# Converting float64 weights to float32 by a scaled copy, shifts and masks, in a fused attention and two-MLP kernel

## The chip, the cores and the metric

The kernel runs on 1 core of one Trainium2 chip. The metric is device time in microseconds: before the change the median of 3 runs is 858.35 us (858.0 to 858.82). Lower is better.

## What is computed

Attention in chunks of 64 tokens (4 batches, 8 heads, 576 tokens, head size 64), then a SiLU MLP (512 to 2048 to 512), then a gated MLP (512 to 1536 to 512), on 2304 tokens. All five weight matrices arrive as float64, and the kernel converts them itself.

```python
scores = scale * np.matmul(q_c, k_c.transpose(0, 1, 2, 4, 3))
attn = np.exp(scores - max); attn = attn / (sum + 1e-09); x = attn @ v_c
h = x @ w_in
x = (h * (1.0 / (1.0 + np.exp(-h)))) @ w_out
out = ((x @ w_a) * (x @ w_b)) @ w_out2
```

## The kernel before

Everything is written out by hand in program order: each engine runs its own instructions in the order in which the source emits them, and nothing is reordered.

**Weights.** A weight block is 128 x 512 float64 (512 KB). There are 68: 32 for the first MLP (16 slices m of the hidden layer, `w_in[m]` and `w_out[m]` in turn, numbered 0 to 31 here, so that block 2m is `w_in[m]`), and 36 for the second. `fetch` (L128) loads a block into one of two raw buffers through SP's queue. `exponents` (L140) takes the sign on ACT, masks the exponent on DVE and rescales it on ACT; `mantissa` (L154) and `begin` (L170) build the mantissa on DVE; `powers` (L182) and `upper` (L187) multiply both together on DVE. For a block of the first MLP `upper` then also rounds the result to the matmul's format on ACT (the upper half, L202), and `lower` (L205) subtracts on DVE what the upper half lost (the lower half, L209). Blocks of the second MLP are written back to DRAM instead. `weights` (L212) chains one block's fetch and opening with the later stages of the block before it.

**Steps.** The first MLP is a loop over steps k; step k = m works on slice m for the first main block of 512 tokens. In one step PE does, in order: the product of slice k+1 with the tokens, `front(k+1)` (12 matmuls of 512 columns: four each of xhi with the upper half of the weights, xlo with the upper half, xhi with the lower half, L384); `side_back(k)` and `side_front(k+1)`, the same work for a side block of 256 tokens, which runs along in the first 16 steps; and `back(k)`, the product with `w_out[k]` (L423). ACT evaluates SiLU on each front twice (L404 and L405), DVE subtracts (L401). Each step calls `prep_a`, and so `weights`, twice: once between `side_back` and `side_front`, once between `side_front` and `back`. Attention for later token tiles is threaded through the steps by a table of steps (`plan`): with the tiles begun at steps 2, 5, 8 and 11 the softmax's exponential falls into steps 3, 6, 9 and 12, between `side_front` and the second `prep_a`.

**The start.** Before step 0 six token tiles go through attention in a hand-ordered sequence, into which blocks 0, 1 and 2 are opened; `busy(n)` (L706) puts n filler matmuls on PE. It ends with `front(0)`, `busy(7)` and `back(0)`.

```python
        finish(pend, 0)
        lower()
        begin_a()
        busy(7)
        back(0)
```

**Buffers.** `tmp` is a set of three 128 x 512 float32 tiles that the mantissas share with SiLU's results `g` until step 17, when mantissas move to a pool of their own (`conv`). `at` is a set of five tiles for attention's q, k, v, scores and probabilities.

Of the kernel before, what the change touches and what calls it, by code (L numbers as in the profile page):

```python
# [7 lines left out]

F32 = mybir.dt.float32
F32R = mybir.dt.float32r  # L10
BF16 = mybir.dt.bfloat16
U16 = mybir.dt.uint16
U32 = mybir.dt.uint32
U64 = mybir.dt.uint64
AF = mybir.ActivationFunctionType
# [5 lines left out]
P = 128  # L21
# [3 lines left out]
def chunk_attention_silu_mlp_gated_mlp(  # L25
# [77 lines left out]
    nc.vector.memset(ebias, -8.0 * ((1023 - 127) << 4))  # L103

    def bank(tag, shape):
        return psum.tile(shape, F32, tag=tag, name="ps_" + tag)
# [18 lines left out]
    turn = [0]  # L125
    leaving = []

    def fetch(src):  # L128
        raw = raws[:, turn[0] % 2]
        turn[0] += 1  # L130
        nc.sync.dma_start(out=raw, in_=src)
        fetched.append(raw)
# [7 lines left out]
    def exponents():  # L140

        raw = fetched.pop(0)
        top = raw.bitcast(U16).rearrange("p (f t) -> p f t", t=4)[:, :, 3]
        topb = raw.bitcast(BF16).rearrange("p (f t) -> p f t", t=4)[:, :, 3]
        e = spool.tile([P, DM], U16, tag="e", name="e")
        sg = spool.tile([P, DM], BF16, tag="sg", name="sg")
        nc.scalar.activation(sg, topb, AF.Sign)  # L147
        nc.vector.tensor_scalar(  # L148
            out=e, in0=top, scalar1=0x7FF0, scalar2=None, op0=ALU.bitwise_and
        )  # L150
        nc.scalar.activation(e, e, AF.Relu, scale=8.0, bias=ebias)  # L151
        opened.append([raw.bitcast(U32).rearrange("p (f t) -> p f t", t=2), e, sg])

    def mantissa():  # L154
        w32 = opened[0][0]
        if "conv" in late:
            mant = late["conv"].tile([P, DM], F32, tag="mant", name="mant", bufs=3)
        else:
            mant = spool.tile([P, DM], F32, tag="tmp", name="mant", bufs=3)
        nc.vector.tensor_scalar(  # L160
            out=mant.bitcast(U32),
            in0=w32[:, :, 1],
            scalar1=0xFFFFF,
            scalar2=0x100000,
            op0=ALU.bitwise_and,
            op1=ALU.bitwise_or,
        )
        opened[0].append(mant)

    def begin(dest):  # L170
        w32, e, sg, mant = opened.pop(0)
        nc.vector.scalar_tensor_tensor(  # L172
            out=mant,
            in0=w32[:, :, 0],
            scalar=2.0**-32,
            in1=mant.bitcast(U32),
            op0=ALU.mult,
            op1=ALU.add,
        )
        stage_1.append((dest, mant, sg, e))  # L180

    def powers():  # L182
        if stage_1:
            _, _, sg, e = stage_1[0]
            nc.vector.tensor_tensor(out=sg, in0=sg, in1=e.bitcast(BF16), op=ALU.mult)

    def upper():  # L187
        if not stage_1:
            return
        dest, w, sg, _ = stage_1.pop()  # L190
        nc.vector.scalar_tensor_tensor(  # L191
            out=w, in0=w, scalar=2.0**-20, in1=sg, op0=ALU.mult, op1=ALU.mult
        )
        if dest[0] == "f":
            wf[dest[1:]] = d = dram.tile([P, DM], F32, name=f"wf{dest[1]}{dest[2]}")
            leaving.append((d, w))
            return
        _, m, j = dest
# [24 lines left out]
    def flush():  # L223
        for _ in range(2):
            lower()
            powers()
            upper()
        leave()

# [162 lines left out]
    def front_a(b, m, ptag, pool, later=False):  # L392
        n = width(b)
        ps = bank(ptag, [P, n])
        product(ps, wA[m][0], x_t[b])
        g = spool.tile([P, DM], F32, tag="tmp", name="g", bufs=3)[:, :n]
        ghi = pool.tile([P, n], F32R, tag="ghi", name="ghi")
        glo = pool.tile([P, n], F32R, tag="glo", name="glo")

        def finish():  # L400
# [54 lines left out]
    def comb_load(u):  # L455
        s, mat = divmod(u, 2)
        if u % 2 and u != 3:
            buf = raws.rearrange("p a n -> p (a n)").bitcast(F32)
        else:
            buf = slot("buf", F32)  # L460
        buf = buf.rearrange("p (o n) -> p o n", o=8)
        for m, sl in ((2 * s, slice(1, 3)), (2 * s + 1, slice(0, 8, 7))):
            nc.gpsimd.dma_start(out=buf[:, sl], in_=wf[mat, m].rearrange("p (o n) -> p o n", o=2))
        bufs[u] = buf
# [182 lines left out]
            units_b += [("f", mat, 2 * s), ("f", mat, 2 * s + 1), ("f", 2, 2 * s + mat)]  # L647
    done = [0, 0]

    def begin_a():  # L650
        begin(("a", *units_a[done[0]]))
        done[0] += 1

    def prep_a():
        if done[0] < len(units_a):
            m, j = units_a[done[0]]
            weights((w_in, w_out)[j][m], ("a", m, j))
            done[0] += 1
            return True
        return False  # L660

    def drain():
        leave()
        lower()
        powers()
        upper()

    def prep_b():
        if done[1] < len(units_b):
# [17 lines left out]
    with tc.manual_schedule():  # L687
# [40 lines left out]

        qk_in(0)
        qk_in(1)  # L730
        fetch(w_in[0])
        v_in(0)
        qk_in(2)
        qk_in(3)
        v_in(1)
        v_in(2)
        fetch(w_out[0])
        v_in(3)
        qk_in(4)
        qk_in(5)  # L740
# [83 lines left out]
        S(1)  # L824
        busy(3)
        att_exp(0)
        exponents()
        S(2)
        att_max(1, W, True)
        att_exp(1)  # L830
        mantissa()
        att_norm(0)
        busy(3)
        Tr(0, "at")
# [11 lines left out]
        rest["X", 0]()  # L846
        rest["P", 1]()
        Tr(2, "sB")
        exponents()
        att_norm(3)  # L850
        rest["P", 2]()
        rest["L", 0]()
# [1 line left out]
        S(4)  # L854
        rest["X", 1]()
        att_max(4, W, True)
        begin_a()
        fetch(w_in[1])
# [6 lines left out]
        powers()  # L865
        rest["X", 2]()
        busy(1)
        mantissa()
        upper()
        S(5)  # L870
        att_norm(4)
# [2 lines left out]
        att_max(5, W)  # L874
        Tr(4, "at")
        rest["P", 4]()
        begin_a()
        lower()
        V(3, "sB")
        rest["X", 3]()  # L880
# [3 lines left out]
        V(4, "sA")  # L884
        rest["X", 4]()
        pend[0], silu = front_a(main[0], 0, "mm", gpool, True)
        powers()
        Tr(5, "at")
        rest["L", 4]()
        silu()  # L890
        rest["P", 5]()
        upper()
        exponents()
        busy(2)
        V(5, "mm")
        mantissa()
        finish(pend, 0)
        lower()
        begin_a()
        busy(7)  # L900
        back(0)
        rest["X", 5]()
        powers()
        upper()
        rest["L", 5]()
        prep_a()
# [8 lines left out]
        first = []  # L915

        def enter_b():
            late.pop("conv")
            conv_cm.__exit__(None, None, None)
            att_cm.__exit__(None, None, None)  # L920
            late["b"] = ctx.enter_context(
                tc.tile_pool(name="bpool", bufs=1, side="right", reuse_waits="tile")
            )
            for h in range(2):
                load_pair(0, h)


        def in_last(m, pos):
            if pos == "c":
                if prep_b():  # L930
                    return
                if leaving or stage_1 or stage_2:
# [134 lines left out]
        for k in range(END):  # L1067
# [8 lines left out]
            run(k, "a2")  # L1076
            if k == MA + 1:
                side_cm.__exit__(None, None, None)
                conv_cm = tc.tile_pool(name="conv", bufs=1, side="right", reuse_waits="tile")
                late["conv"] = conv_cm.__enter__()  # L1080
            if k in joint:
                finish(pend, k + 1)
            if k >= L0:
# [250 lines left out]
```

## Time and profile before

| | us |
|---|---|
| median of 3 runs | 858.35 |
| the profiled execution, its own time | 858.17 |
| its span in the profile | 856.4 |
| PE busy | 846.9 |
| DVE busy | 571.4 |
| ACT busy | 440.9 |

The profiled execution took 858.17 us, of which the span of the profile covers 856.4. PE is busy for 99% of it; of the 40 slices of the page only the first and the last show PE busy for less than nine tenths. Mean granted clock of TensorE over the span is 0.997 of full speed.

### The profile page before, as it was taken

The numbers are of one execution on the slowest core, as the hardware profiler recorded it, in microseconds if no ns is written. First come the engines' busy times: TensorE is split into PE (matmuls) and PEld (weight loads), VectorE is DVE, ScalarE is ACT, GpSimd is POOL, SyncE is SP. The second block draws the span as 40 slices with busy tenths as digits, with TensorE's granted clock in tenths as the row PEclk, the third lists the DMA queues.
The fourth block names the chain that finished last, engine by engine and source line by source line (L and its number), as shares of the span: only waits on it lengthen the run. The fifth ranks groups of instructions, "written<-read, shape, count | busy, mean of one in ns | idle before, by whom it ended". The sixth has DMA issues, their size and how long they took to land.

```text
span 856.4 us, 14161 instructions
## 1 busy us (share of the span) xinstructions
PE 846.9 (99%) x5484; PEld 771.6 (90%) x5484; DVE 571.4 (67%) x1097; ACT 440.9 (51%) x837; POOL 50.3 (6%) x91
## 2 busy tenths in 40 slices
PE   8999999999999999999999999999999999999998
PEld 7788888888888888888889999999999999999998
DVE  6996977765677656766865998583554594454563
ACT  6777767745665656545555554363333373333252
POOL 0000000020100100023201110000000000000000
PEclk9999999999999999999999999999999999999999
DMA  7454443355554655457799788878766888666761
GB/s 271 119 179 134 145 152 111 100 181 200 166 187 152 222 172 161 160 184 290 252 364 370 295 314 328 308 293 269 258 258 263 304 299 281 241 250 247 290 227 56
DMA packets 54034, 193.85 MB, mean 226 GB/s; under 512 B 5904, under 2 KB 13584, under 8 KB 45520
## 3 DMA queue, kind: packets, MB, share of 16 engines
q1 hardware_dynamic: 46752, 169.76, 55.6%
q0 software_dynamic: 6928, 22.81, 8.1%
q8 instruction: 43, 0.70, 0.3%
q10 hardware_dynamic: 288, 0.39, 0.1%
q14 instruction: 23, 0.19, 0.1%
HBM read 141.03 MB, written 51.90 MB: 225 GB/s over the span
## 4 chain that ended last, share of the span: by engine, by line
PE 95%; ACT 2%; issue 1%; DVE 1%; DMA 1%; SPq 0%; ACTq 0%
PE ps_acc L980 23%; PE ps_acc L423 20%; PE ps_mm L384 15%; PE ps_sA L384 7%; PE ps_at L980 6%; PE ps_sA L980 6%; PE ps_mm L980 5%; PE ps_sB L980 5%; PE ps_sA L423 2%; PE ps_sB L423 1%; PE ps_at L384 1%; PE ps_at L267 1%; PE ps_at L349 1%; PE ps_at L326 1%; DMA start<-kt 1%
## 5 line engine op out<-in xcount | busy, mean ns | idle before, releaser
L980 PE MATMUL ps_acc<-xo,ring 128*128 128x384 f32 x868 | 168.2, 335 | 0.0
L423 PE MATMUL ps_acc<-ghi,wA 128*128 128x512 f32 x512 | 159.2, 392 | 0.0
L980 PEld LDWEIGHTS ps_acc<-xo,ring 128*128 128x128 f32 x868 | 152.0, 188 | 0.3 <-DVE gq L1055 0.3
L423 PEld LDWEIGHTS ps_acc<-ghi,wA 128*128 128x128 f32 x512 | 94.2, 188 | 19.1
L384 PE MATMUL ps_mm<-xhi,wA 128*128 128x512 f32 (+1 forms) x400 | 100.7, 373 | 0.0
L423 PE MATMUL ps_acc<-glo,wA 128*128 128x512 f32 x256 | 100.0, 390 | 0.0
L384 PEld LDWEIGHTS ps_mm<-xhi,wA 128*128 128x128 f32 x400 | 70.6, 188 | 12.6 <-ACT wA L202 0.2
L401 DVE TENSOR_TENSOR glo<-g,ghi 128x512 fp32r<-128x512 f32 x80 | 50.5, 632 | 31.4 <-ACT ghi L405 31.4
L404 ACT ACTIVATE g<-ps_mm 128x512 f32<-128x512 f32 (+1 forms) x50 | 28.0, 559 | 81.7 <-PE ps_mm L384 76.7
L423 PEld LDWEIGHTS ps_acc<-glo,wA 128*128 128x128 f32 x256 | 48.0, 188 | 10.2
L1114 ACT ACTIVATE u<-gq 128x384 fp32r<-128x384 f32 x84 | 40.6, 516 | 30.4 <-DVE gq L1055 28.6
L1115 DVE TENSOR_TENSOR u<-gq,u 128x384 fp32r<-128x384 f32 x84 | 44.4, 552 | 17.4 <-ACT u L1114 17.0
L980 PE MATMUL ps_acc<-u,ring 128*128 128x384 f32 x272 | 53.6, 337 | 0.3
L151 ACT ACTIVATE e<-e,ebias 128x512 uint16<-128x512 uint16 x68 | 49.1, 722 | 9.1 <-DVE e L148 9.1
L384 PE MATMUL ps_mm<-xlo,wA 128*128 128x512 f32 (+1 forms) x200 | 49.8, 371 | 0.0
L384 PE MATMUL ps_sA<-xhi,wA 128*128 128x512 f32 x184 | 49.6, 391 | 0.0
L980 PEld LDWEIGHTS ps_acc<-u,ring 128*128 128x128 f32 x272 | 47.6, 188 | 1.3 <-ACT gq L989 0.8
L980 PE MATMUL ps_at<-xo,ring 128*128 128x384 f32 x231 | 47.8, 334 | 0.0
L191 DVE SCALAR_TENSOR_TENSOR mant<-mant,sg 128x512 f32<-128x512 f32 x68 | 46.5, 684 | 0.1
L172 DVE SCALAR_TENSOR_TENSOR mant<-raws,mant 128x512 f32<-128x512 uint32 x68 | 46.5, 683 | 0.1
L147 ACT ACTIVATE sg<-raws 128x512 bf16<-128x512 bf16 x68 | 45.7, 672 | 0.6 <-DMA raws<-w_in 0.6
L980 PE MATMUL ps_sB<-xo,ring 128*128 128x384 f32 x220 | 44.9, 334 | 0.0
(185 smaller groups left out, 1490.1 us busy)
## 6 DMA issues: line engine op xcount, KB each, us to landing
ring<-w SPq DMA_DIRECT2D x30, 1024.0 KB, 6.3
ring<-wg SPq DMA_DIRECT2D x24, 1024.0 KB, 4.9
ring<-wg SPq DMA_DIRECT2D x24, 768.0 KB, 5.7
wg<-ring SPq DMA_DIRECT2D x12, 1024.0 KB, 6.6
wf<-mant SPq DMA_DIRECT2D x36, 256.0 KB, 2.2
wg<-ring SPq DMA_DIRECT2D x12, 768.0 KB, 6.4
raws<-w_in SPq DMA_DIRECT2D x16, 512.0 KB, 3.5
raws<-w_out SPq DMA_DIRECT2D x16, 512.0 KB, 3.5
```

Source lines behind the costliest of these rows:

```text
L147: nc.scalar.activation(sg, topb, AF.Sign)
L151: nc.scalar.activation(e, e, AF.Relu, scale=8.0, bias=ebias)
L172: nc.vector.scalar_tensor_tensor(out=mant, in0=w32[:, :, 0], scalar=2.0**-32, in1=mant.bitcast(U32), op0=ALU.mult, op1=ALU.add,)
L191: nc.vector.scalar_tensor_tensor(out=w, in0=w, scalar=2.0**-20, in1=sg, op0=ALU.mult, op1=ALU.mult)
L267: nc.tensor.matmul(soft[i][j % len(soft[i])][n, j, hp, :], lhsT=q[r, hp, n], rhs=k[r, hp, n], start=True, stop=True,)
L384: nc.tensor.matmul(ps, lhsT=a[:, kk * P:(kk + 1) * P], rhs=b[:, kk, :], start=(j == 0 and kk == 0), stop=(j == 2 and kk == KT - 1),)
L401: nc.vector.tensor_tensor(out=glo, in0=g, in1=ghi.bitcast(F32), op=ALU.subtract)
L404: nc.scalar.activation(g, ps, AF.Silu)
L423: nc.tensor.matmul(acc_t[b][j], lhsT=a[:, j * P:(j + 1) * P], rhs=g, start=(m == 0 and i == 0 and (b != SIDE or j % 2 == 0)), stop=(m == M ...
L980: nc.tensor.matmul(ps, lhsT=a, rhs=b, start=first and i == 0, stop=last and i == 2, skip_group_check=True,)
L1114: nc.scalar.activation(hi, src, AF.Copy)
L1115: nc.vector.tensor_tensor(out=lo, in0=src, in1=hi.bitcast(F32), op=ALU.subtract)
```

## The change

**Conversion.** `scaled` makes one ACT instruction of a block: a copy, times 2^111, of the upper 32-bit words of the raw float64, read as float32. `magnitude` multiplies it on DVE by two constants in one instruction and, in a second one in place, shifts left by 3 and masks the sign. `begin` puts the sign bit in from the raw upper words and then the three leading bits of the raw lower words, two DVE instructions in place. `exponents`, `mantissa`, `powers` and the multiplication in `upper` are gone. `upper` keeps only the rounding on ACT, `lower` is as it was.

**Stages.** In `weights` each stage now works on a block one call behind the stage ahead of it: a call that fetches block n scales it at its end, brings block n-1 through `magnitude` and `begin`, and block n-2 through `upper` and `lower`. Before, a call opened and began block n, ran `powers` and `upper` for n-1 and `lower` for n-2.

**Buffers.** There are three raw buffers. `g` no longer takes a `tmp` tile during the first MLP: the side block has a tile of its own, the main block holds one `at` tile until step 17 and uses a pool of two tiles (`gate`) after that; the pool `conv` is gone.

**Fillers.** `busy(7)` ahead of `back(0)` is `busy(2)`.

```diff
-    raws = spool.tile([P, 2, DM], U64, tag="raw", name="raws", bufs=1)
+    raws = spool.tile([P, RAWS, DM], U64, tag="raw", name="raws", bufs=1)
...
+    def scaled():
+        dest, raw = fetched.pop(0)
+        w = spool.tile([P, DM], F32, tag="tmp", name="w", bufs=3)
+        nc.scalar.activation(w, words(raw)[1].bitcast(F32), AF.Copy, scale=2.0**111)
+        opened.append((dest, raw, w))
+
+    def magnitude():
...
+        w = opened[0][2]
         nc.vector.tensor_scalar(
+            out=w, in0=w, scalar1=2.0**-126, scalar2=2.0**-97, op0=ALU.mult, op1=ALU.mult
         )
         nc.vector.tensor_scalar(
+            out=w.bitcast(U32), in0=w.bitcast(U32), scalar1=3, scalar2=0x7FFFFFFF,
+            op0=ALU.logical_shift_left, op1=ALU.bitwise_and,
         )
+    def begin():
...
         nc.vector.scalar_tensor_tensor(
+            out=wu, in0=high, scalar=0x80000000, in1=wu,
+            op0=ALU.bitwise_and, op1=ALU.bitwise_or,
         )
         nc.vector.scalar_tensor_tensor(
+            out=wu, in0=low, scalar=29, in1=wu,
+            op0=ALU.logical_shift_right, op1=ALU.bitwise_or,
         )
...
     def weights(src, dest):
-        fetch(src)
         leave()
-        exponents()
+        fetch(src, dest)
+        upper()
+        magnitude()
+        begin()
         lower()
-        powers()
-        mantissa()
-        upper()
-        begin(dest)
+        scaled()
...
-        g = spool.tile([P, DM], F32, tag="tmp", name="g", bufs=3)[:, :n]
+        if b == SIDE:
+            g = side.tile([P, n], F32, tag="g", name="g")
+        elif "g" in late:
+            g = late["g"].tile([P, n], F32, tag="g", name="g", bufs=2)
+        elif "b" in late:
+            g = spool.tile([P, n], F32, tag="tmp", name="g", bufs=3)
+        else:
+            if "g1" not in late:
+                late["g1"] = late["att"].tile([P, DM], F32, tag="at", name="g")
+            g = late["g1"]
...
-        lower()
-        begin_a()
-        busy(7)
+        magnitude()
+        begin()
+        busy(2)
         back(0)
         rest["X", 5]()
-        powers()
         upper()
         rest["L", 5]()
         prep_a()
         prep_a()
```

How the order of instructions changes, at the three places that matter below. Numbers behind a name tell its tiles apart.

ACT in step 0, before: the product `front(2)` reads the weight tile `wA_698` (block 4), and L202 fills its upper half.

```order
L404 ACTIVATE g_668<-ps_mm_655 128x512
L405 ACTIVATE ghi_669<-ps_mm_655 128x512
L147 ACTIVATE sg_689<-raws_82 128x512
L151 ACTIVATE e_688<-e_688,ebias_80 128x512
L202 ACTIVATE wA_698<-mant_631 128x512
L404 ACTIVATE g_715<-ps_at_702 128x256
L405 ACTIVATE ghi_716<-ps_at_702 128x256
```

ACT in step 0 now: `front(2)` reads `wA_687`, and L196 is the upper half; `g_683` and `ghi_681` are the SiLU of `side_front(1)`.

```order
L399 ACTIVATE g_535<-ps_mm_627 128x512
L400 ACTIVATE ghi_640<-ps_mm_627 128x512
L196 ACTIVATE wA_594<-w_599 128x512
L147 ACTIVATE w_665<-raws_82 128x512
L399 ACTIVATE g_683<-ps_at_668 128x256
L400 ACTIVATE ghi_681<-ps_at_668 128x256
L196 ACTIVATE wA_687<-w_606 128x512
```

The upper half that `front(2)` needs stood ahead of the side block's SiLU and now stands behind it.

ACT in step 3, before: `front(5)` writes `ps_mm_1033` and reads `wA_976` (block 10); L297 is the exponential of attention.

```order
L202 ACTIVATE wA_976<-mant_909 128x512
L404 ACTIVATE g_999<-ps_mm_986 128x256
L405 ACTIVATE ghi_1000<-ps_mm_986 128x256
L297 ACT_TABLE_LOAD
L297 ACTIVATE s_979<-s_979 128x512
L147 ACTIVATE sg_1009<-raws_82 128x512
L151 ACTIVATE e_1008<-e_1008,ebias_80 128x512
L202 ACTIVATE wA_976<-mant_973 128x512
L404 ACT_TABLE_LOAD
L404 ACTIVATE g_1046<-ps_mm_1033 128x512
```

ACT in step 3 now: `front(5)` writes `ps_mm_969` and reads `wA_947`.

```order
L399 ACTIVATE g_940<-ps_mm_925 128x256
L400 ACTIVATE ghi_938<-ps_mm_925 128x256
L283 ACT_TABLE_LOAD
L283 ACTIVATE s_918<-s_918 128x512
L196 ACTIVATE wA_947<-w_857 128x512
L147 ACTIVATE w_954<-raws_82 128x512
L399 ACT_TABLE_LOAD
L399 ACTIVATE g_535<-ps_mm_969 128x512
```

The upper half of block 10 stood ahead of the side block's SiLU, the table load and the exponential, and now stands behind all of them; what stood behind them before was that of block 11, which `back(5)` reads a step later.

DVE at the start, before: the lines ahead of the last `xlo` (L365, from `ps_sB`) that `front(0)` reads.

```order
L286 TENSOR_TENSOR start<-ps_acc_444,mx 128x4x64
L286 TENSOR_TENSOR start<-ps_acc_445,mx 128x4x64
L172 SCALAR_TENSOR_TENSOR mant<-raws,mant 128x512
L209 TENSOR_TENSOR wA<-mant,wA 128x512
L365 TENSOR_TENSOR xlo<-ps_sB,xhi 128x4x128
```

DVE at the same place now, where that `xlo` is L351.

```order
L272 TENSOR_TENSOR start<-ps_acc_437,mx 128x4x64
L272 TENSOR_TENSOR start<-ps_acc_438,mx 128x4x64
L174 SCALAR_TENSOR_TENSOR w<-raws,w 128x512
L178 SCALAR_TENSOR_TENSOR w<-raws,w 128x512
L203 TENSOR_TENSOR wA<-w,wA 128x512
L351 TENSOR_TENSOR xlo<-ps_sB,xhi 128x4x128
```

One more instruction stands ahead of `xlo`, and it reads what the one ahead of it writes.

## Rows read from the trace of the kernel before

**Rows 1.** The page, part 1: busy us, share of the span, instructions.

```profile
PE 846.9 (99%) x5484; PEld 771.6 (90%) x5484; DVE 571.4 (67%) x1097; ACT 440.9 (51%) x837; POOL 50.3 (6%) x91
```

**Rows 2.** Stretches: length, busy PE, PEld, DVE, ACT, POOL, granted clock, DMA.

```profile
30.00:40.00 10.00, 9.49 (x85) 8.20 (x84) 9.93 (x21) 7.34 (x13) 0.00 (x0) 1.00 0.29 76
```

**Rows 3.** Groups by line and form: count, busy us, mean ns, idle before.

```profile
L151 ACT ACTIVATE e<-e,ebias 128x512 uint16<-128x512 uint16 x68 | 49.1, 722 | 9.1 <-DVE e L148 9.1
...
L172 DVE SCALAR_TENSOR_TENSOR mant<-raws,mant 128x512 f32<-128x512 uint32 x68 | 46.5, 683 | 0.1
L147 ACT ACTIVATE sg<-raws 128x512 bf16<-128x512 bf16 x68 | 45.7, 672 | 0.6 <-DMA raws<-w_in 0.6
...
L160 DVE TENSOR_SCALAR mant<-raws 128x512 uint32<-128x512 uint32 x68 | 28.5, 419 | 0.0
...
L202 ACT ACTIVATE wA<-mant 128x512 fp32r<-128x512 f32 x32 | 20.3, 633 | 8.5 <-DVE mant L191 8.5
```

**Rows 4.** Timeline of DVE, steps 2 and 3: start us, us, instruction.

```profile
63.91 0.69 DVE L191 SCALAR_TENSOR_TENSOR mant<-mant,sg 128x512 f32<-128x512 f32 x1
64.51 0.68 DVE L172 SCALAR_TENSOR_TENSOR mant<-raws,mant 128x512 f32<-128x512 uint32 x1
66.32 0.69 DVE L281 TENSOR_REDUCE mx<-ps_at 128x8 f32<-128x512 f32 x1 [1.13 <-PE ps_at L267]
67.05 0.69 DVE L286 TENSOR_TENSOR s<-ps_at,mx 128x512 f32<-128x512 f32 x1
```

**Rows 5.** The chain that ended last, at the start: start us, us, what.

```profile
17.42 0.34 DVE e L148
```

**Rows 6.** Timeline of the start, DVE and PE, up to `back(0)`.

```profile
26.57 0.68 DVE L172 SCALAR_TENSOR_TENSOR mant<-raws,mant 128x512 f32<-128x512 uint32 x1
...
27.77 0.68 DVE L365 TENSOR_TENSOR xlo<-ps_sB,xhi 128x512 fp32r<-128x512 f32 x1
...
28.51 1.20 PE L384 MATMUL ps_mm<-xlo,wA 128*128 128x512 f32 x4
...
32.94 0.68 DVE L209 TENSOR_TENSOR wA<-mant,wA 128x512 fp32r<-128x512 f32 x1
...
33.36 1.83 PE L710 MATMUL ps_sA<-start 128*128 128x128 f32 x14
...
34.95 0.70 PE L423 MATMUL ps_acc<-ghi,wA 128*128 128x512 f32 x2
```

**Rows 7.** Timeline, end of step 0: upper half, last third of `side_front(1)`, `front(2)`.

```profile
44.34 0.64 ACT L202 ACTIVATE wA<-mant 128x512 fp32r<-128x512 f32 x1
44.41 0.64 PE L384 MATMUL ps_at<-xhi,wA 128*128 128x256 f32 x4
...
45.04 1.19 PE L384 MATMUL ps_mm<-xhi,wA 128*128 128x512 f32 x4
```

**Rows 8.** Timeline, step 3: last third of `side_front(4)`, ACT, then `front(5)`.

```profile
68.70 0.64 PE L384 MATMUL ps_mm<-xhi,wA 128*128 128x256 f32 x4
...
69.66 0.38 ACT L405 ACTIVATE ghi<-ps_mm 128x256 fp32r<-128x256 f32 x1
70.06 1.28 ACT L297 ACT_TABLE_LOAD   x1
71.35 0.63 ACT L297 ACTIVATE s<-s 128x512 f32<-128x512 f32 x1
71.89 0.65 ACT L147 ACTIVATE sg<-raws 128x512 bf16<-128x512 bf16 x1
...
71.91 1.07 PE L384 MATMUL ps_mm<-xhi,wA 128*128 128x512 f32 x4
```

**Rows 9.** Tile k, POOL's loads; timeline of PE, transposes, then the next scores.

```profile
DMA to landing us min/median/max: 3.2/3.8/6.1
...
80.28 0.60 PE L326 MATMUL ps_at<-ident,s 128*128 128x128 f32 x4
...
86.26 0.68 PE L267 MATMUL ps_at<-k,q 64*64 64x64 f32 x16
```

More of the change, by code (lines that the diff above doesn't have):

```diff
@@ L126, in chunk_attention_silu_mlp_gated_mlp, with fetch @@
     leaving = []
-    def fetch(src):
-        raw = raws[:, turn[0] % 2]
+    def fetch(src, dest):
+        raw = raws[:, turn[0] % RAWS]
         turn[0] += 1
         nc.sync.dma_start(out=raw, in_=src)
-        fetched.append(raw)
+        fetched.append((dest, raw))
     def leave(n=0):
@@ L138, in leave, with words @@
             nc.sync.dma_start(out=dst, in_=src)
[L140 to L147, printed above, removed]
+    def words(raw):
+        w32 = raw.bitcast(U32).rearrange("p (f t) -> p f t", t=2)
+        return w32[:, :, 0], w32[:, :, 1]
@@ L148, in exponents @@
+    def scaled():
[4 more added lines that the diff above has]
+    def magnitude():
+        if not opened:
+            return
+        w = opened[0][2]
         nc.vector.tensor_scalar(
-            out=e, in0=top, scalar1=0x7FF0, scalar2=None, op0=ALU.bitwise_and
+            out=w, in0=w, scalar1=2.0**-126, scalar2=2.0**-97, op0=ALU.mult, op1=ALU.mult
@@ L150, in exponents @@
         )
[L151 to L159, printed above, removed]
-        nc.vector.tensor_scalar(
[L161 to L166, printed above, removed]
-        )
-        opened[0].append(mant)
@@ L170, in begin @@
-    def begin(dest):
-        w32, e, sg, mant = opened.pop(0)
-        nc.vector.scalar_tensor_tensor(
[L173 to L178, printed above, removed]
-        )
[L180 to L190, printed above, removed]
+        nc.vector.tensor_scalar(
+            out=w.bitcast(U32),
+            in0=w.bitcast(U32),
+            scalar1=3,
+            scalar2=0x7FFFFFFF,
+            op0=ALU.logical_shift_left,
+            op1=ALU.bitwise_and,
+        )
@@ L191, in upper @@
+    def begin():
+        if not opened:
+            return
+        dest, raw, w = opened.pop(0)
+        low, high = words(raw)
+        wu = w.bitcast(U32)
+        nc.vector.scalar_tensor_tensor(
+            out=wu, in0=high, scalar=0x80000000, in1=wu,
+            op0=ALU.bitwise_and, op1=ALU.bitwise_or,
+        )
         nc.vector.scalar_tensor_tensor(
-            out=w, in0=w, scalar=2.0**-20, in1=sg, op0=ALU.mult, op1=ALU.mult
+            out=wu, in0=low, scalar=29, in1=wu,
+            op0=ALU.logical_shift_right, op1=ALU.bitwise_or,
@@ L196, in upper @@
             leaving.append((d, w))
+        else:
+            stage_1.append((dest, w))
+    def upper():
+        if not stage_1:
             return
+        dest, w = stage_1.pop()
         _, m, j = dest
@@ L212, in weights @@
     def weights(src, dest):
-        fetch(src)
         leave()
-        exponents()
+        fetch(src, dest)
+        upper()
+        magnitude()
+        begin()
         lower()
-        powers()
-        mantissa()
-        upper()
-        begin(dest)
-    def flush():
-        for _ in range(2):
-            lower()
-            powers()
-            upper()
-        leave()
+        scaled()
     qk = {}
@@ L648, in chunk_attention_silu_mlp_gated_mlp, with next_a @@
     done = [0, 0]
-    def begin_a():
-        begin(("a", *units_a[done[0]]))
+    def next_a():
+        m, j = units_a[done[0]]
         done[0] += 1
+        return (w_in, w_out)[j][m], ("a", m, j)
     def prep_a():
         if done[0] < len(units_a):
-            m, j = units_a[done[0]]
-            weights((w_in, w_out)[j][m], ("a", m, j))
-            done[0] += 1
+            weights(*next_a())
             return True
@@ L663, in drain @@
         leave()
+        upper()
+        magnitude()
+        begin()
         lower()
-        powers()
-        upper()
     def prep_b():
@@ L730, in chunk_attention_silu_mlp_gated_mlp @@
         qk_in(1)
-        fetch(w_in[0])
+        fetch(*next_a())
         v_in(0)
@@ L736, in chunk_attention_silu_mlp_gated_mlp @@
         v_in(2)
-        fetch(w_out[0])
+        fetch(*next_a())
         v_in(3)
@@ L826, in chunk_attention_silu_mlp_gated_mlp @@
         att_exp(0)
-        exponents()
+        scaled()
         S(2)
@@ L856, in chunk_attention_silu_mlp_gated_mlp @@
         att_max(4, W, True)
-        begin_a()
-        fetch(w_in[1])
+        begin()
+        fetch(*next_a())
         Tr(3, "sA")
@@ L876, in chunk_attention_silu_mlp_gated_mlp @@
         rest["P", 4]()
-        begin_a()
+        begin()
         lower()
@@ L886, in chunk_attention_silu_mlp_gated_mlp @@
         pend[0], silu = front_a(main[0], 0, "mm", gpool, True)
-        powers()
+        upper()
         Tr(5, "at")
         rest["L", 4]()
+        lower()
         silu()
         rest["P", 5]()
-        upper()
-        exponents()
+        scaled()
         busy(2)
         V(5, "mm")
-        mantissa()
         finish(pend, 0)
-        lower()
-        begin_a()
-        busy(7)
+        magnitude()
+        begin()
+        busy(2)
         back(0)
         rest["X", 5]()
-        powers()
         upper()
@@ L917, in enter_b @@
         def enter_b():
-            late.pop("conv")
-            conv_cm.__exit__(None, None, None)
+            late.pop("g")
+            g_cm.__exit__(None, None, None)
             att_cm.__exit__(None, None, None)
@@ L1078, in chunk_attention_silu_mlp_gated_mlp @@
                 side_cm.__exit__(None, None, None)
-                conv_cm = tc.tile_pool(name="conv", bufs=1, side="right", reuse_waits="tile")
-                late["conv"] = conv_cm.__enter__()
+                g_cm = tc.tile_pool(name="gate", bufs=1, side="right", reuse_waits="tile")
+                late["g"] = g_cm.__enter__()
             if k in joint:
```

17 lines of the change are left out of this document (8 added, 9 removed).

## The prediction

> **What bounds the kernel now.** I read the page first, then busy time by stretches, then the chain that ended last, and then the timeline at the places that the chain passes. PE is busy for 846.9 of 856.4 us [rows 1], so a lighter DVE or ACT is worth nothing by itself: time can be won only where PE has no work, which is in the first 35 us, and lost wherever PE begins to wait. Just ahead of `back(0)` DVE is the fullest engine, with 9.93 of 10 us [rows 2], and PE fills what it lacks with fillers. From 35 us on PE runs from product to product. So two questions decide: when does `back(0)` start, and does any product after it wait for something it did not wait for before? Times here are made against the profiled execution, 858.17 us (span 856.4); the median of the runs is 0.18 higher. A measurement of this kernel tells some 0.2%, 1.7 us, from no change.
>
> **The price of a conversion.** Before, a block costs ACT a sign of 0.67 and a rescaling of 0.72 us [rows 3]; now it costs one copy, for which I take the 0.63 of the copy at L202, with the 0.67 of L147, which also reads with a stride, as the other bound. On DVE three instructions near 0.42 (like L160) and two near 0.68 (like L172) [rows 3] become two of the first and two of the second size. For the multiplication by two constants on float32 no row stands in the trace: it lies between 0.42, one input of 32-bit words, and 0.68, two inputs [rows 3]. I take 0.42, as it has one input, and keep +0.26 an instruction for the range. By busy time DVE saves 0.42 us a block, but not by the clock on the wall. Two neighbours on DVE that don't touch the same tile start 0.60 apart (63.91 to 64.51), though each takes 0.68; where the second reads what the first writes it starts 0.73 after (66.32 to 67.05) [rows 4]. All four new instructions work in place on one tile, each on the result of the one ahead, so a block takes about 0.45 + 0.45 + 0.72 + 0.60 = 2.2 us, as much as the five before (3 x 0.33 + 2 x 0.60 = 2.2). DVE is not relieved. The Trainium skill, "VectorE: DVE Perf Modes", § Rules for kernel authors, says of chained DVE operations that a flush happens regardless and that one should minimize the count of operations, not semaphores. The rows above speak against that here. By that rule the step from the first to the second of a pair would cost 0.60 and not 0.72, and the sum below would be 0.1 us less.
>
> **The start, up to `back(0)`.** Three edits.
> Fillers: 14 records of `busy(7)` run from 33.36 to 34.95 [rows 6], 0.114 each, and ten go: **-1.1 us**. They lie on the path: `back(0)` follows right behind, and the last thing that it reads, the lower half of block 1, is done at 32.94 + 0.68 = 33.62 [rows 6], over a microsecond before it starts.
> The exponent mask at 17.42 held the chain for 0.34 us [rows 5]; it goes, and with it 0.34 at most. I keep **-0.2**, as the scores that DVE works on next come from PE, which gets no earlier.
> `front(0)` waits at 28.51 for the last `xlo`, 27.77 to 28.45. Ahead of it stands L172 at 26.57 [rows 6]. Now two instructions that depend on each other stand where L172 stood, which puts one more step of 0.72 in front: `xlo` ends at 28.45 - 0.2 + 0.72 = 28.97 and the second third of `front(0)` starts near 29.03, not 28.51. This delay hands itself on through SiLU, the last tile's transposes and its values to the fillers: the two together **+0.5**. Bounds: 0.4 if all of the 0.34 comes through, +1.0 if the float32 multiplication is slow. `back(0)` then starts at 34.4 and not at 34.95.
> Third raw buffer: SP can issue the fetch of block 2 earlier. No row shows the start waiting for that fetch, so it gives nothing.
>
> **Step 0.** `front(2)` now finds its upper half late. Before, L202 made it (44.34 to 44.98) ahead of the side block's SiLU, and `front(2)` started at 45.04, almost at once behind the last third of `side_front(1)`, which starts at 44.41 [rows 7]. Now the same upper half stands on ACT behind that SiLU, and the SiLU needs `side_front(1)`. Step 3 shows how long that takes: the last third of the side front starts at 68.70, the second SiLU ends at 70.04 [rows 8]; the next instruction on ACT may start 0.09 before such an end (71.89 against 71.98), so 1.25 after the third began. Then 0.64 for the upper half and 0.06 to PE (44.98 to 45.04): 44.41 + 1.95 = 46.36 in place of 45.04: **+1.3 us**. In later steps `back(k)` stands between the side front and the next front and gives ACT 71.91 - 68.70 = 3.2 us where it needs 1.95, so there the later place is free. Step 0 alone has no `back`, since `back(0)` ran at the start.
>
> **Steps 3, 6, 9 and 12.** There that cover is spent. Behind the SiLU ACT loads a table (70.06 to 71.34) and runs attention's exponential from 71.35; what comes next starts at 71.89 [rows 8]. That was a sign nobody waited for. Now it is the upper half for `front(5)`: done at 71.89 + 0.63 = 72.52, at PE by 72.58, where `front(5)` started at 71.91: 0.67 us. And the first weight load is then no longer hidden: the four matmuls behind a wait took 1.19 [rows 7], those without one 1.07 [rows 8]. So 0.79 a step, and the four steps repeat the pattern: **+3.2 us**. The exponential itself can't move ahead: it needs the table, and the table waits for the SiLU. The lower half follows on DVE right after, one instruction of 0.68, and only the last third of the front reads it, so it adds nothing.
>
> **What costs nothing.** DVE's in-order wait for the new place of `upper` in both calls holds back `g`'s subtraction and the softmax's maximum; the first is read a step later, the second only when the table load has ended. The single `g` tile of the main block must be read before the next SiLU, a whole step away. Moving `leave` ahead of `fetch` on SP: the raw data of a fetch are needed a call later. From step 14 on no product waits for a conversion, so the second MLP's 36 blocks change nothing. POOL's load of k for the next tile now waits for the transposes, as one of the five `at` tiles is taken: transposes end at 80.88, landing takes 3.8 in the median, so 84.7, and the scores start at 86.26 [rows 9]. Hidden by 1.5 us; at the longest landing, 6.1, it would be 0.75 late, at three tiles.
>
> **Sum.** 858.17 - 1.1 + 0.5 + 1.3 + 3.2 = **862.1 us**, 0.45% slower. Bounds of the unknown costs: 861.3 (all of the 0.34, no cost of dependence, weight loads hidden in the four steps, so 0.67 each) to 862.6 (slow multiplication).
>
> **Rivals.**
> *ACT is in time.* If the upper half reached PE before the next front in the four steps and in step 0, only the start would count: 858.17 - 1.1 + 0.5 = 857.6, no change that can be told. It decides at one point, whether ACT gets from the side front's end to the upper half's end within 3.2 us. For it: ACT loses 0.75 us a block and stands idle for much of a step. Against it: that saving lies ahead of the SiLU, which waits for PE anyway, and the price from SiLU to upper half is made of rows alone.
> *The start is bound by busy time* (the other side). DVE is 99% busy there [rows 2]; if the four instructions ran at their busy time, three blocks would save 3 x 0.42 = 1.3 us on top of the fillers, and if in addition the waits above were covered, the time is 858.17 - 1.1 - 1.3 = 855.8, faster. It decides by the spacing of dependent neighbours on DVE: at 0.60 it holds, at 0.73 [rows 4] it doesn't.
> *k comes late.* With landings near 6.1 in all three tiles [rows 9], 3 x 0.75 = 2.2 more: 864.3. For it: the load moves from ahead of the step to behind the transposes. Against it: the median leaves 1.5 us.
>
> **How the numbers follow.** The forecast gets 0.73, k late 0.10 (both slower by over 0.2%), ACT in time 0.12 (within), the busy-time start 0.05 (faster). The likeliest case's own range is 861.3 to 862.6. Upward the range takes in k late; downward it goes to a mixed case, the low prices with ACT in time in two of the four steps, 858.17 - 1.1 + 0.2 + 1.3 + 2 x 0.67 = 859.9, and leaves out the two rivals below, 0.17: 859.9 to 864.3.
>
> **What would show it.** Right: in the timeline `front(2)` waits over 1 us for ACT's `wA`, and the fronts behind the table load in steps 3, 6, 9 and 12 wait 0.6 to 0.8 us each; the fillers ahead of `back(0)` are four records and `back(0)` starts near 34.4; a block's four DVE instructions span 2.2 us. Wrong: no idle time of PE ahead of those fronts, `back(0)` before 33.9 or after 35, or PE waiting for POOL's k at the scores.

## The result, and the profile after

The changed kernel takes 862.7 us (median of 6 runs, 862.34 to 863.83) against 858.23 us before (6 runs): a ratio of 1.0053, 95% interval 1.0040 to 1.0066. The forecast was 862.1 us, with a range of 859.9 to 864.3. Two of the eleven runs of one kernel below (before, `busy(2)`, two more raw buffers) took 1193 and 1694 us, the profiled one among them, so its time is the median of the other nine and its profile isn't read.

The span of the profiled execution grew from 856.4 to 860.9 us, 4.5 us, while PE's busy time hardly moved [rows 1]: PE waits more. The page, part 1, of the changed kernel:

```profile
PE 846.5 (98%) x5474; PEld 769.5 (89%) x5474; DVE 566.7 (66%) x1029; ACT 398.5 (46%) x769; POOL 50.2 (6%) x91
```

ACT lost 42 us of work and DVE 5, and the kernel is slower. Groups by line and form (count, busy us, mean ns, idle before), which answer to [rows 3]:

```profile
L174 DVE SCALAR_TENSOR_TENSOR w<-raws,w 128x512 uint32<-128x512 uint32 x68 | 47.1, 692 | 2.3
L178 DVE SCALAR_TENSOR_TENSOR w<-raws,w 128x512 uint32<-128x512 uint32 x68 | 47.1, 692 | 2.3
L147 ACT ACTIVATE w<-raws 128x512 f32<-128x512 f32 x68 | 45.5, 670 | 16.6 <-DMA raws<-w_b 8.8 <-DMA raws<-w_a 6.2 <-DMA raws<-w_o 1.5
L158 DVE TENSOR_SCALAR w<-w 128x512 uint32<-128x512 uint32 x68 | 29.1, 427 | 2.3
L155 DVE TENSOR_SCALAR w<-w 128x512 f32<-128x512 f32 x68 | 28.6, 421 | 7.0 <-ACT w L147 7.0
```

The float32 multiplication (L155) takes 421 ns: the lower bound, which the forecast took. The scaled copy (L147) takes 670, the upper bound.

PE's program is the same in both kernels but for ten filler records, so each matmul's place in one trace can be set against its place in the other. Where the difference changes:

| | predicted | measured |
|---|---|---|
| `back(0)` starts | -0.6 (34.4) | -0.62 (34.33) |
| step 0 | +1.3 | +1.14 |
| steps 3, 6, 9, 12 | 4 x 0.79 | 0.75, 0.78, 0.78, 0.79 |
| near 521 us, in the second MLP | nothing | +0.77 |
| sum | +3.9 | +4.5 (0.1 of it small changes elsewhere) |

The start, timeline of DVE and PE (start us, us, instruction), answering to [rows 6]:

```profile
26.34 0.68 DVE L174 SCALAR_TENSOR_TENSOR w<-raws,w 128x512 uint32<-128x512 uint32 x1
27.06 0.69 DVE L178 SCALAR_TENSOR_TENSOR w<-raws,w 128x512 uint32<-128x512 uint32 x1
27.21 1.20 PE L370 MATMUL ps_mm<-xhi,wA 128*128 128x512 f32 x4
28.27 0.68 DVE L351 TENSOR_TENSOR xlo<-ps_sB,xhi 128x512 fp32r<-128x512 f32 x1
29.01 1.20 PE L370 MATMUL ps_mm<-xlo,wA 128*128 128x512 f32 x4 [0.59 <-DVE xlo L351]
33.87 0.71 PE L705 MATMUL ps_sA<-start 128*128 128x128 f32 x4
34.33 0.71 PE L418 MATMUL ps_acc<-ghi,wA 128*128 128x512 f32 x2
```

The dependent pair L174, L178 is 0.72 apart and the last `xlo` ends at 28.95 (28.97 was forecast). PE waits 0.59 for it. The four filler records left take 0.46 us.

In the kernel before, PE starts `front(0)` here, in its first and in a second profile:

```profile
27.44 1.19 PE L384 MATMUL ps_mm<-xhi,wA 128*128 128x512 f32 x4
27.21 1.21 PE L384 MATMUL ps_mm<-xhi,wA 128*128 128x512 f32 x4
```

So from the start of `front(0)` to `back(0)` it is 7.12 us now and was 7.51: 0.73 more for the wait on `xlo`, 1.11 less for the fillers. The other 0.23 of the 0.62 was won ahead of `front(0)`, and the second profile of the unchanged kernel wins it too, so it can't be told from the scatter of single executions.

Step 0, timeline, answering to [rows 7]:

```profile
43.78 0.64 PE L370 MATMUL ps_at<-xhi,wA 128*128 128x256 f32 x4
44.73 0.38 ACT L400 ACTIVATE ghi<-ps_at 128x256 fp32r<-128x256 f32 x1
44.99 0.63 ACT L196 ACTIVATE wA<-w 128x512 fp32r<-128x512 f32 x1
45.68 1.20 PE L370 MATMUL ps_mm<-xhi,wA 128*128 128x512 f32 x4 [1.27 <-ACT wA L196]
46.73 0.68 DVE L203 TENSOR_TENSOR wA<-w,wA 128x512 fp32r<-128x512 f32 x1
47.64 0.63 PE L370 MATMUL ps_mm<-xhi,wA 128*128 128x512 f32 x2
```

`front(2)` starts 1.90 after the last third of `side_front(1)` (1.95 was forecast), 1.27 of them a wait for the upper half. Note L203: the lower half is done at 47.41, and the third that reads it starts at 47.64. Hardly a quarter of a microsecond lies between.

Step 3, timeline, answering to [rows 8]:

```profile
69.22 0.64 PE L370 MATMUL ps_mm<-xhi,wA 128*128 128x256 f32 x4
70.57 1.28 ACT L283 ACT_TABLE_LOAD   x1
71.87 0.63 ACT L283 ACTIVATE s<-s 128x512 f32<-128x512 f32 x1
72.41 0.61 ACT L196 ACTIVATE wA<-w 128x512 fp32r<-128x512 f32 x1
73.07 1.19 PE L370 MATMUL ps_mm<-xhi,wA 128*128 128x512 f32 x4 [0.48 <-ACT wA L196]
```

From the side front's last third to `front(5)` it is 3.85 us; before, it was 3.21 [rows 8]. The first four matmuls take 1.19 and not 1.07, which with the 0.64 of delay is 0.76.

And one place that the forecast didn't have, timeline of DVE and PE:

```profile
520.91 0.43 DVE L487 TENSOR_TENSOR raws<-raws 128x256 f32<-128x256 f32 x1 [0.67 <-DMA raws<-wf]
525.57 1.34 PE L972 MATMUL ps_acc<-xo,ring 128*128 128x384 f32 x6 [0.61 <-DVE gq L1047]
```

The same two instructions before:

```profile
516.47 0.42 DVE L492 TENSOR_TENSOR raws<-raws 128x256 f32<-128x256 f32 x1
521.12 1.32 PE L980 MATMUL ps_acc<-xo,ring 128*128 128x384 f32 x6
```

DVE now waits for a transfer into the raw buffers, and a product of the second MLP waits for DVE. Before, neither waited: the transfer had landed at 515.0.

### The profile page after: what moved, and what is told of

It reads as the page before. It is cut to its first block, busy times and chain, and to the rows that moved or that the text cites. A ratio compares the mean times of both kernels' runs of the same rounds, so it can differ in the third digit from the quotient of the medians.

```text
span 860.9 us, 14124 instructions
## 1 busy us (share of the span) xinstructions
PE 846.5 (98%) x5474; PEld 769.5 (89%) x5474; DVE 566.7 (66%) x1029; ACT 398.5 (46%) x769; POOL 50.2 (6%) x91
## 4 chain that ended last, share of the span: by engine, by line
PE 86%; issue 5%; ACT 3%; DMA 3%; DVE 3%; POOL 0%; POOLq 0%; ACTq 0%; DVEq 0%
PE ps_acc L972 19%; PE ps_acc L418 19%; PE ps_mm L370 15%; PE ps_sA L370 7%; PE ps_at L972 5%; PE ps_sA L972 5%; PE ps_sB L972 4%; PE ps_mm L972 4%; DMA raws<-wf 2%; PE ps_sA L418 1%; PE ps_sB L418 1%; PE ps_at L370 1%; PE ps_at L253 1%; PE ps_at L335 1%; PE ps_sA L705 1%
## 5 line engine op out<-in xcount | busy, mean ns | idle before, releaser
L147 ACT ACTIVATE w<-raws 128x512 f32<-128x512 f32 x68 | 45.5, 670 | 16.6 <-DMA raws<-w_b 8.8
L178 DVE SCALAR_TENSOR_TENSOR w<-raws,w 128x512 uint32<-128x512 uint32 x68 | 47.1, 692 | 2.3
L174 DVE SCALAR_TENSOR_TENSOR w<-raws,w 128x512 uint32<-128x512 uint32 x68 | 47.1, 692 | 2.3
L972 PE MATMUL ps_sA<-xo,ring 128*128 128x384 f32 x213 | 44.4, 335 | 0.1
```

What stands on the lines that cost most here:

```text
L147: nc.scalar.activation(w, words(raw)[1].bitcast(F32), AF.Copy, scale=2.0**111)
L174: nc.vector.scalar_tensor_tensor(out=wu, in0=high, scalar=0x80000000, in1=wu, op0=ALU.bitwise_and, op1=ALU.bitwise_or,)
L178: nc.vector.scalar_tensor_tensor(out=wu, in0=low, scalar=29, in1=wu, op0=ALU.logical_shift_right, op1=ALU.bitwise_or,)
L972: nc.tensor.matmul(ps, lhsT=a, rhs=b, start=first and i == 0, stop=last and i == 2, skip_group_check=True,)
```

## The experiments

Each kernel was timed against the kernel before on its chip (857.76 to 858.09 us there). The ratio is worked out over all of these runs and differs from the quotient of two medians by up to 0.0005. One figure helps in reading profiles: the changed kernel and the five that differ from it only behind that place start the second third of `front(0)` between 28.79 and 29.83 us in single profiled executions. So places are compared from that point on.

| kernel | us | ratio to before, 95% interval |
|---|---|---|
| changed | 862.70 | 1.0053, 1.0040 to 1.0066 |
| upper half ahead, all steps | 859.32 | 1.0019, 1.0010 to 1.0028 |
| upper half ahead, steps 3, 6, 9, 12 | 859.68 | 1.0022, 1.0013 to 1.0031 |
| upper half ahead, step 0 | 863.30 | 1.0060, 1.0047 to 1.0073 |
| both halves ahead | 858.14 | 1.0001, 0.9993 to 1.0010 |
| changed, `busy(7)` | 863.20 | 1.0060, 1.0046 to 1.0074 |
| changed, two raw buffers | 862.48 | 1.0054, 1.0042 to 1.0067 |
| changed, ten records ahead of `S(2)` | 862.20 | 1.0046, 1.0034 to 1.0059 |
| before, `busy(2)` | 858.77 | 1.0009, 1.0000 to 1.0018 |
| before, `busy(2)`, two more raw buffers | 858.17 | 1.0001, 0.9992 to 1.0011 |
| the same, ten records ahead of `S(2)` | 857.49 | 0.9995, 0.9986 to 1.0004 |
| before again | 857.98 | 0.9999, 0.9989 to 1.0008 |
| the best version | 856.96 | 0.9986, 0.9977 to 0.9995 |

### The late upper half: all steps, the four steps, step 0

```diff
+            if k < MA:
+                upper()
             side_front(k + 1)
             run(k, "c2")
```

> The changed kernel with the second upper half of a step (L196) issued ahead of side_front's SiLU instead of behind it, in every step of the first MLP; all else as changed. Theory (the late upper half): the wait ahead of front(2) (1.27 us) and the four ahead of the fronts in steps 3, 6, 9 and 12 (0.64 to 0.79 each) go, 1.15 + 3.1 = 4.25 us: 862.7 becomes 858.4 to 858.5, within 0.1% of the kernel before. Rival (the new conversion itself holds PE up, by its chain of four dependent DVE instructions): the halves come no earlier, the waits stay or move to L203, and the time stays within 1 us of 862.7. If in addition PE's wait of 0.8 us near 521 us of the profile, for a transfer into raws, was of one execution only, the time is 857.7.

```diff
             side_front(k + 1)
+            if (k, "c2") in todo:
+                upper()
             run(k, "c2")
```

> The changed kernel with the upper half ahead of the table load and the exponential in steps 3, 6, 9 and 12 only (still behind the side block's SiLU). Theory: the four waits go and that of step 0 stays, 862.7 - 3.1 = 859.6. Rival (the table load and exponential are no cause; ACT would be late behind the SiLU alone): less than 1 us is won.

```diff
+            if k == 0:
+                upper()
             side_front(k + 1)
```

> The changed kernel with the upper half ahead of side_front's SiLU in step 0 only. Theory: front(2) starts right behind side_front(1), 1.15 us are won, 861.5; the four later waits stay. Rival: if step 0 waits for the conversion's DVE part (L178 ends 42.18) and not for the order on ACT, nothing is won.

The four steps are as the theory has them. Timeline of step 3, ACT and PE, of the second of these kernels, with the upper half ahead of the table load:

```profile
71.28 0.64 ACT L196 ACTIVATE wA<-w 128x512 fp32r<-128x512 f32 x1
71.93 1.28 ACT L283 ACT_TABLE_LOAD   x1
73.26 1.07 PE L370 MATMUL ps_mm<-xhi,wA 128*128 128x512 f32 x4
```

No wait, and 1.07 for the four matmuls. The four steps give back 3.1 us in the profile, and the ratio falls by 0.0031, 2.7 us.

Step 0 is not. Its repair alone gains nothing (1.0060), and with all steps repaired step 0 is only 0.05 us shorter by the profile. The timeline of step 0 with the upper half ahead in all steps, DVE and PE:

```profile
46.68 0.69 DVE L203 TENSOR_TENSOR wA<-w,wA 128x512 fp32r<-128x512 f32 x1
47.41 1.20 PE L370 MATMUL ps_mm<-xhi,wA 128*128 128x512 f32 x4 [0.99 <-DVE wA L203]
```

`front(2)` starts in time now, and its last third waits 0.99 us for the lower half, which stands on DVE behind the four conversions of the next block. Two waits lay one behind the other, and either alone costs nearly the whole; the profile of the changed kernel shows only the first. For the repair of step 0 alone the number is the rival's, nothing won, but not its cause: the upper half comes in time there too.

### Both halves ahead

The first experiment, and on DVE the lower half and the side block's `glo` ahead of the next conversions (`finish` is not called again below while k < MA):

```diff
             run(k, "c2")
+            if k < MA:
+                lower()
+                finish(side_g, k + 1)
```

> The changed kernel with the second upper half of a step ahead of side_front's SiLU, as in the first experiment, and with its lower half (L203) and the side block's glo (L396) ahead of the four conversions of the next block on DVE. Theory (behind the upper half it was the lower half, in DVE's queue behind those four, that front(2) waited for, 0.99 us before its last third): that wait goes, step 0 has none, and 859.3 becomes 858.2 to 858.4. Rival (the queue on DVE hands the delay to what now stands behind, glo or the halves of step 1): 859.3, with a new wait in step 0 or 1.

858.14 us, 1.2 less than with the upper half alone, and as fast as the kernel before. Timeline of step 0, PE and DVE:

```profile
44.15 1.19 PE L370 MATMUL ps_mm<-xhi,wA 128*128 128x512 f32 x4
44.26 0.69 DVE L203 TENSOR_TENSOR wA<-w,wA 128x512 fp32r<-128x512 f32 x1
46.10 1.07 PE L370 MATMUL ps_mm<-xhi,wA 128*128 128x512 f32 x4
```

No wait is left in step 0, nor in steps 3, 6, 9 and 12. So within the steps the conversion by scaled copy costs PE nothing; the order of its stages did. That the whole kernel is level with the one before is a balance: the ten fillers that went (1.1 us) pay for what the change still costs, the 0.7 at the last `xlo` of `front(0)` and some 0.4 near 521 us, where PE waits 0.26.

### The fillers alone, in either kernel

```diff
-        busy(7)
+        busy(2)
         back(0)
```

> The kernel before with busy(2) in place of busy(7) ahead of back(0), and nothing else. Theory (the fillers lie on the path): ten records of 0.11 us go, back(0) starts 1.1 us earlier, 858.2 - 1.1 = 857.1. Rival (the fillers cover a wait for block 1's lower half or for glo): back(0) waits instead, and less than half of that is won.

Less than half is won, as the rival has it, but not for its reason: 858.77 us, 0.8 slower by the ratio if anything, and `back(0)` doesn't wait. It does start 1.1 us earlier (counted from `front(0)`), and by 49 us all of it is gone. Timeline, ACT and PE:

```profile
38.68 0.67 ACT L147 ACTIVATE sg<-raws 128x512 bf16<-128x512 bf16 x1 [0.73 <-DMA raws<-w_in]
42.15 0.60 ACT L404 ACTIVATE g<-ps_mm 128x512 f32<-128x512 f32 x1 [0.55 <-DVE glo L401]
45.31 1.19 PE L384 MATMUL ps_mm<-xhi,wA 128*128 128x512 f32 x4 [0.31 <-ACT wA L202]
49.01 0.38 PE L423 MATMUL ps_sA<-glo,wA 128*128 128x256 f32 x1 [0.43 <-DVE glo L401]
```

ACT waits for a raw block that could be fetched only when a raw buffer came free, SiLU waits for a tile that DVE still reads, and PE waits for both. Then the wait of DVE and PE near 521 us shows here too, 0.61 and 0.55.

The other way round, the changed kernel with `busy(7)`:

> The changed kernel with busy(7) back in place of busy(2), and nothing else. Theory (in the changed kernel the path from back(0) on is PE's own, through front(1), its SiLU and the halves behind it, so fillers count in full): 862.7 + 1.1 = 863.8, ratio to before about 0.13% above that of the changed kernel. Rival (as in the kernel before, where taking ten records out won nothing, PE is caught up with before front(2) by conversions that come at their own time): no change, 862.7, and the wait ahead of front(2) is shorter by as much as back(0) is later.

```profile
46.82 1.20 PE L370 MATMUL ps_mm<-xhi,wA 128*128 128x512 f32 x4 [1.27 <-ACT wA L196]
521.30 0.42 DVE L487 TENSOR_TENSOR raws<-raws 128x256 f32<-128x256 f32 x1
```

In the timeline `front(2)` starts 1.14 us later with the same wait of 1.27: here the fillers count in full, as in the theory, up to 520 us. But L487 no longer waits, and 0.77 us come back. By the profile 0.38 us remain; the ratios of the two kernels can't be told apart.

### Raw buffers

Blocks 3 and 4 of the kernel before, with `busy(2)`, in buffers of their own:

```diff
         raw = raws[:, turn[0] % 2]
+        if turn[0] in (3, 4):
+            if "raw" not in shared:
+                shared["raw"] = slot("start", F32)
+            h = turn[0] % 2
+            raw = shared["raw"][:, h * 2 * DM:(h + 1) * 2 * DM].bitcast(U64)
```

> The kernel before with busy(2), and two more raw buffers for blocks 3 and 4 alone (they lie in a tile that nothing else uses then), so that SP fetches those blocks without waiting for a raw buffer that the conversion of an earlier one holds. Theory (with two raw buffers the fetch of block 4 at 34 to 35 us, its landing 3.5 us later, and the sign, mask and rescaling behind it set when step 0's SiLU and halves come; this took the fillers' gain back): ACT no longer waits for raws at 37.7, PE no longer waits for wA and glo at 45 and 49, and 1.1 us less than the kernel before: 857.76 - 1.1 = 856.7. Rival (DVE's own work sets it): the waits stay, and the time is that of the kernel before or a little over.

858.17 us, a ratio of 1.0001: the time that the rival has. Of this kernel only the time is read; the kernel under "Both, in the kernel before" repeats it with ten records more, and has a profile.

The changed kernel with two raw buffers (`RAWS = 2`):

> The changed kernel with two raw buffers in place of three. Theory (a raw buffer is held one call longer now, so with two the fetch of block 4 goes from 27.8 us back to 35.7 us and lands at 39.2, when ACT is about to read it): a delay of 0 to 0.5 us in step 0, 862.7 to 863.2. Rival (the third buffer is what keeps each step's conversions in time): ACT waits for raws in many steps, and 2 us or more are lost.

862.48 us, and step 0 ends where it did: the third raw buffer is worth nothing in the changed kernel, as forecast.

### The wait near 521 us

Before again, unchanged:

> The kernel before, unchanged, for a second profile and as a control. If PE's wait of 0.3 to 0.6 us near 521 us, seen in all five profiles since the change and not in the one of before, belongs to single executions, it shows here too; if it is the changed timing's, this profile has none. The ratio is 1.000 within its interval.

Its profile has no such wait. The ten records put back at a place where PE waits anyway, in the changed kernel:

```diff
         S(1)
-        busy(3)
+        busy(8)
```

> The changed kernel with busy(8) in place of busy(3) ahead of S(2), where PE waits 1.5 to 2.8 us for a load anyway: ten filler records more at a place where they cost nothing, so that PE's program again has as many instructions ahead of step 0 as before. Theory (ten records fewer moved the point at which a packet of 16 KB of the instruction queue is loaded, from 1 us ahead of the transfer into raws at 511 us to 3 to 4 us behind its issue, and the transfer lands later): PE's wait near 525 us (0.61, and 0.33 to 0.55 in the other kernels with busy(2)) is gone, 0.7 us won, 862.0. Rival (that wait is the times' own, from the order of transfers): it stays, 862.7.

The wait is gone; 0.0007 of the ratio is less than its interval, so the gain in time (0.5 us) is by the profile: 0.77 near 521 us, less 0.3 at 146.5 us, where PE waits 0.25 for a load of attention's `k`. The DMA view tells more. Its row of the instruction queue q8 (packets, MB, share), for the changed kernel from 511.4 to 520, behind the issue of the transfer at 511.48:

```profile
q8 instruction: 1, 0.02, 0.9%
```

For the kernel before, second profile, from 505.2 to 507.6, ahead of the issue at 507.67:

```profile
q8 instruction: 1, 0.02, 2.4%
```

And for the changed kernel with the ten records back, from 509.6 to 512, ahead of the issue at 512.09:

```profile
q8 instruction: 1, 0.02, 2.5%
```

In the 2.4 us ahead of the issue the changed kernel has no such packet, and in the 8.6 us behind it the other two have none. The two transfers land 7.4 us after issue in the median in the changed kernel, 5.5 in the kernel before (6.0 in its first profile) and 6.2 with the ten records back.

### Both, in the kernel before

> The kernel before with busy(2) ahead of back(0), raw buffers of their own for blocks 3 and 4, and the ten records put back ahead of S(2). Theory (two things took the fillers' gain back: the fetch that waits for a raw buffer, worth 1.1 us at step 0, and the place of the instruction load, worth 0.5 to 0.7 us): both gone, 1.1 us less than the kernel before, 856.7, ratio 0.9987. Rival (DVE's chain sets step 0 whatever the fetch does): ratio 1.000.

857.49 us, a ratio of 0.9995, between theory and rival. No wait near 521 us, and ACT no longer waits for `raws`. But of the 1.12 us by which `back(0)` starts earlier 0.40 are left behind step 0. Timeline, ACT and PE:

```profile
40.77 0.60 ACT L409 ACTIVATE g<-ps_mm 128x512 f32<-128x512 f32 x1 [0.55 <-DVE glo L406]
47.30 0.39 PE L428 MATMUL ps_sA<-glo,wA 128*128 128x256 f32 x1 [0.43 <-DVE glo L406]
```

SiLU still waits for a tile that `g` shares with the mantissas, and DVE's own queue is late. So the fetch took some 0.4 us of the 1.1, and DVE with the shared tiles the rest; these two weren't tried apart.

### The best version

Both halves ahead, `busy(8)` ahead of `S(2)`, and at the start:

```diff
-        begin()
         lower()
         V(3, "sB")
...
         att_norm(5)
+        begin()
...
-        upper()
         Tr(5, "at")
         rest["L", 4]()
-        lower()
         silu()
         rest["P", 5]()
+        upper()
+        lower()
```

> The changed kernel with the halves ahead as in the experiment on both halves, the ten records ahead of S(2) as in the two kernels sent with it, and at the start begin() of block 1 moved behind the softmax of the last tile, its upper and lower half behind the SiLU of front(0). Theory (one dependent DVE instruction ahead of the last xlo cost 0.5 us; block 1's halves have time until back(0)): the second third of front(0) waits no more, back(0) starts 0.5 to 0.7 us earlier, the wait near 521 us goes (0.3), 858.1 - 0.9 = 857.2, ratio to before 0.9990. Rival (the start is bound elsewhere, or block 1's halves now come late to back(0)): ratio 0.9997 to 1.0005.

```profile
27.25 1.08 PE L370 MATMUL ps_mm<-xlo,wA 128*128 128x512 f32 x4
32.66 0.71 PE L418 MATMUL ps_acc<-ghi,wA 128*128 128x512 f32 x2
112.40 0.68 PE L253 MATMUL ps_at<-k,q 64*64 64x64 f32 x16 [0.27 <-DMA k<-kt]
```

The timeline of PE shows the second third of `front(0)` without a wait and `back(0)` 1.67 us earlier than in the changed kernel; 0.99 of this is there already when `front(0)` starts, and 0.68 is the edit's. 856.96 us, a ratio of 0.9986 (0.9977 to 0.9995): 1.1 us faster than the kernel before, and the only kernel here whose interval lies below 1. From the start of `front(0)` to `back(0)` it is 1.07 us shorter than the kernel before, as much as the ten fillers took: by this profile the gain is theirs, and the conversion itself about breaks even.

The last line shows a new wait. In the changed kernel POOL's `k` lands 1.1 to 1.3 us ahead of the scores of its three tiles; here it takes 4.6 to 5.0 us to land and not 3.5 to 3.7, the margin is 0.2 us or less, and about 0.4 us of the gain is lost. What delays it wasn't tried.

## Why the prediction was right, and where it was not

**Bound and place.** Right: PE's own work didn't change, the difference is waits of PE and the slower start of the matmuls behind them, and 42 us of ACT's time bought nothing.

**The conversion's price.** Right: on DVE the four instructions start 0.47, 0.46 and 0.72 apart, and the next follows 0.61 later, 2.26 us (2.2 was forecast). The Trainium skill, "VectorE: DVE Perf Modes", § Rules for kernel authors, has it that the number of operations counts and semaphores don't; here the last of the four follows 0.72 behind the one whose result it reads and is followed after 0.61 by one that is independent of it, so a dependent step costs 0.11 more, and here the measurement speaks against the rule.

**The start.** Right where it rests on rows: ten of 14 filler records gone (1.11), one DVE step of 0.72 put ahead of `xlo`. That `back(0)` at 34.33 also agrees to 0.1 us is partly luck: kernels with the same start have it between 34.11 and 35.16, and the -0.2 for the exponent mask isn't shown by any run, as the unchanged kernel's second profile starts `front(0)` just as early.

**Step 0.** The size was right (1.3 forecast, 1.14 in the end), the reason only half, so the size is partly luck. "Now the same upper half stands on ACT behind that SiLU" is what the trace shows, but taking that away won nothing: the lower half on DVE comes 0.23 us before it is needed, and would cost nearly as much alone. That the lower half "adds nothing" was written of steps 3 to 12, where it holds; for step 0 the forecast gave it no price, and there the four conversions that stand ahead of it on DVE make it late as well.

**Steps 3, 6, 9 and 12.** Right in place, mechanism and size: 3.1 us measured, and 3.1 given back when the upper half goes ahead of the table load.

**Costs at nothing.** The third raw buffer, `g`'s tile, the leave ahead of the fetch: right, no wait of PE names them. POOL's `k`: the forecast left it a margin of 1.5 us, and it was 1.1 to 1.3, so PE doesn't wait for it in the changed kernel and that rival fell. But the margin is thin: in two later kernels PE does wait for `k`, 0.25 and 0.27 us. The busy-time start fell by the 0.72 of the dependent pair. ACT in time fell by the waits themselves.

**What was missing.** The fillers were priced as time alone. In the changed kernel taking ten out is worth 1.1 us at `back(0)`, and costs 0.77 us at 521 us in its profile (0.4 to 0.7 in the others), by where an instruction load falls. The step that had no such term is "so the second MLP's 36 blocks change nothing": it asks what waits for a conversion, not what a shift in time does to a transfer. The trace of before has the transfer landing 1.5 us ahead of its reader (515.0 and 516.47). The 0.77 accounts for the difference between 862.1 and 862.7. And in the kernel before the same edit is worth nothing, as step 0 takes it back. Which part of the change keeps the gain there (`g`'s own tile, or stages a call apart) wasn't tried apart; the third raw buffer isn't it.

## What to carry to other kernels

When a pipeline is cut into more stages, look up for each consumer what now stands ahead of the last stage on its engine: here the stage that made the operand slid behind a table load and an exponential, and one call that moves it back recovers 2.7 us. When a wait is removed, find the second wait at the same product before counting on the gain: a profile shows only the one that PE comes to first, and here the next lay 0.23 us behind it. And a filler in front of the path is a gain only as far as the next thing that doesn't depend on it.

## What the runs showed of the hardware

Ten PE records fewer at 34 us moved a wait into 521 us. In the seven profiles read with ten records fewer, of either kernel, PE waits 0.25 to 0.61 us there and the packet of q8 comes 4.0 to 4.3 us behind the issue of the transfer into the raw buffers; in the six with as many as before, whether at their old place or at a new one, it comes within 0.5 us ahead of the issue and PE doesn't wait. The Trainium skill, "Runtime: NRT & Kernel Launch", § Instruction fetch mechanics, says that instructions are fetched in 16 KiB blocks by a DMA queue of the sequencer and that this is mostly hidden. The packet of 0.02 MB (16384 bytes) agrees with such a block; in six of the thirteen profiles it is hidden, in seven it isn't. That the load delays the transfer by sharing the DMA engines is inferred from the times; it wasn't measured by itself.
